# Reordering group 0 by hand and pairing the tiles of the two-chunk groups in a fused retention and snake-MLP kernel

## The chip, the cores and the metric

The kernel runs on one core of one Trainium2 chip. The metric is the device time in microseconds of one execution; ten runs of the kernel before are given by their median. Beside it stands one execution taken by the hardware profiler.

## The reference, cut to what matters

```python
# q, k, v: 4 batches, 8 heads, 768 steps, 64 wide
for t in range(S):
    state = gamma * state + k[:, :, t] (outer) v[:, :, t]
    y[:, :, t] = scale * q[:, :, t] @ state
x = y.transpose(0, 2, 1, 3).reshape(B * S, H * D)      # 3072 x 512
h = x @ w_in                                           # 512 x 2048
s = np.sin(alpha * h)
g = h + s * s / (alpha + 1e-09)
out = g @ w_out                                        # 2048 x 512
```

`gamma` is one decay factor per head, so that the recurrence can be worked in chunks of 128 steps: a masked product inside each chunk and a running state between chunks.

## The kernel before

**Tiles.** The 3072 rows are 24 chunks of 128 (four batches of six). `order` (L47) puts the first chunk of each batch in front, then the other chunks batch by batch; `P` is the same list, `e0` to `e3` are its first four. `sizes` (L49) cuts it into seven groups of 4, 2, 4, 4, 4, 4 and 2 chunks.

**Retention stages of a chunk j.** `stage_T` (L190) transposes q and k on TensorE and copies the result from PSUM to SBUF on DVE; for later chunks `turn` (L199) does this by a DMA transpose from SyncE's queue instead. `stage_A` (L204) makes the scores and DVE multiplies them by the mask (L214). `stage_M` (L233) makes the chunk's x from state and scores, adds to the state (`stage_S`, L217), and `keep_S` (L228) copies the state to SBUF with two ACT instructions. `scale_v` (L111) multiplies v by its decay, on DVE for a few chunks and on POOL for the others.

**MLP stages of a group g.** For each of 16 tiles f of the hidden width, `ff_in` (L262) runs four matmuls into a PSUM bank `ph`, then ACT's sine (L272) and a square (L274 on ACT, or L276 on DVE) and, when the returned function is called, DVE's add (L277), which makes `gT`. `ff_out` (L284) runs one matmul of 512 columns for one chunk ts and one f; after f = 15 it copies the 128x512 result with ACT and sends it out from SyncE's queue (L298).

**What sets the order.** The schedule is written out by hand (L60): each engine runs its instructions in the order in which the program emits them. `phase` (L357) emits for each f an `ff_in`, the retention stages attached to that f in `att`, the add, and a share of the output matmuls of the group before. Group 0 is written out (L391 to L454): its first six tiles f run for three chunks alone while the fourth chunk is still arriving, with the matmuls of `idle_work` (L307, on data that nobody reads) between; then the fourth chunk's 128 columns follow tile by tile; then ten tiles of all four chunks, with squares in turn on ACT and DVE. Output tile 0 trails them; the other three follow between the stages of chunks P[4] and P[5] (`fill`, L427). Then comes group 1's phase (L455), and the loop over groups 2 to 6 (L458).

**Banks and buffers.** PSUM is shared by tags: `mm` has four banks, for `ph`, `po` and early transposes; `ty`, `ps` and `pa` serve the retention stages. A new tile of a tag waits until the oldest one's readers are done. `s` has four buffers in SBUF.

**Loads.** Everything that needs a cast comes through POOL's DMA queue, in program order: first chunks, w_in and w_out in four pieces each (L117 to L125), chunks P[4] to P[6], then (L432) the other chunks, with the scaling of v between the loads. SyncE's queue holds the DMA transposes and the outputs.

```python
    for n in range(7, NJ + 3):
        if n > 8:
            scale_v(order[n - 3], nc.gpsimd)
        if n < NJ:
            load_chunk(order[n])
        if n in (13, 15, 17):
            scale_v(order[(n - 11) // 2], nc.gpsimd)
```

Of the kernel before, what the change touches and what calls it, by code (L numbers as in the profile page):

```python
# [15 lines left out]
def kernel(  # L16
# [15 lines left out]
    nc = tc.nc  # L32
# [40 lines left out]
    def load_chunk(j, names="qkv"):  # L73
        for name, src in (("q", q), ("k", k), ("v", v)):
            if name not in names:
                continue
            if name == "v":
                t = big.tile([128, H, D], BF16, name="vr", tag="vr", bufs=NJ)
            else:
                if ("qk", j) not in raw:  # L80
                    raw["qk", j] = big.tile([128, 2, H, D], BF16, name="qkr", tag="qkr", bufs=NJ)
                t = raw["qk", j][:, "qk".index(name)]
            nc.gpsimd.dma_start(out=t, in_=chunk_of(src, j))  # L83
            raw[name, j] = t
# [26 lines left out]
    def scale_v(j, eng):  # L111
        eng.tensor_mul(raw["v", j], raw["v", j], kg[:, j % NCH, :, None].to_broadcast([128, H, D]))  # L112
# [51 lines left out]
    def decay_table(c):  # L164
        nc.vector.tensor_mul(qg[:, c], qg[:, 0], step[:, c, :, None].to_broadcast([128, NP, C]))
# [21 lines left out]
        else:  # L187
            nc.vector.tensor_copy(o, pt)

    def stage_T(j):  # L190
        pt = psum.tile([128, 2 * NP, 128], BF16, name="pt", tag="ty")
        st["qkT", j] = work.tile([128, 2 * NP, 128], BF16, name="qkT", tag="qkT", bufs=6)
        for i in range(2):
            for p in range(NP):
                nc.tensor.transpose(pt[:, i * NP + p, :],
                                    raw["qk"[i], j][:, 2 * p:2 * p + 2, :].rearrange("p h d -> p (h d)"), ident)
        nc.vector.tensor_copy(st["qkT", j], pt)

    def turn(j):  # L199

# [3 lines left out]
    def stage_A(j):  # L204
        qkT = st["qkT", j]
        pa = psum.tile([128, 2, NP, 128], F32, name="pa", tag="pa")
        for p in range(NP):
            for e in range(2):
                r = slice(64 * e, 64 * e + 64)
                nc.tensor.matmul(pa[:, e, p, :], qkT[r, NP + p, :], qkT[r, p, :],  # L210
                                 start=(p == 0), stop=True, skip_group_check=True)
        aT = work.tile([128, 2, NP, 128], BF16, name="aT", tag="aT", bufs=2)
        m = dec.rearrange("p e n t -> p (e n) t") if j % NCH == 0 else mask_bc
        nc.vector.tensor_mul(aT.rearrange("p e n t -> p (e n) t"), pa.rearrange("p e n t -> p (e n) t"), m)  # L214
        st["aT", j] = aT
# [43 lines left out]

    gT = {}  # L260

    def ff_in(g, f, square, cols=None):  # L262
        n = sizes[g] * C
        lo, hi = cols or (0, n)
        if g not in gT:
            gT[g] = work.tile([128, FF, n], BF16, name="gT", tag="gT", bufs=2)
        ph = psum.tile([128, hi - lo], F32, name="ph", tag="mm", bufs=4)
        s = work.tile([128, hi - lo], F32, name="s", tag="s", bufs=4)
        for i in range(KS):
            nc.tensor.matmul(ph, w_in[:, i, f * 128:(f + 1) * 128], xT[g][:, i, lo:hi],  # L270
                             start=(i == 0), stop=(i == KS - 1))
        nc.scalar.activation(out=s, in_=ph, func=ACTF.Sin, scale=alpha_sb[:, f:f + 1])  # L272
        if square == "A":
            nc.scalar.activation(out=s, in_=s, func=ACTF.Square)  # L274
        else:
            nc.vector.tensor_mul(s, s, s)  # L276
        return lambda: nc.vector.scalar_tensor_tensor(  # L277
            gT[g][:, f, lo:hi], s, rec_alpha[:, f:f + 1], ph, op0=ALU.mult, op1=ALU.add)

    out_view = out.rearrange("(t p) n -> p t n", p=128)  # L280
    po = {}
    end = (NG - 1, sizes[-1] - 1)

    def ff_out(g, ts, f):  # L284
        if f == 0:
            po[g, ts] = psum.tile([128, d_model], F32, name="po", tag="mm", bufs=4)
        nc.tensor.matmul(po[g, ts], gT[g][:, f, ts * C:(ts + 1) * C], w_out[:, f, :],  # L287
                         start=(f == 0), stop=(f == FF - 1))
        if f == FF - 1:
            o_sb = work.tile([128, d_model], F32, name="o_sb", tag="o_sb", bufs=3)  # L290
            o_dram = out_view[:, groups[g][ts], :]
            if (g, ts) == end:
                h = d_model // 2
                nc.vector.tensor_copy(o_sb[:, :h], po[g, ts][:, :h])
                nc.scalar.copy(o_sb[:, h:], po[g, ts][:, h:])
            else:
                nc.scalar.copy(o_sb, po[g, ts])  # L297
            nc.sync.dma_start(out=o_dram, in_=o_sb)  # L298

    def out_pieces(g, tss):  # L300
        return [lambda ts=ts, f=f: ff_out(g, ts, f) for ts in tss for f in range(FF)]
# [5 lines left out]
    def idle_work(n):  # L307
        for _ in range(n):
            nc.tensor.matmul(spare["ps"], warm[:, :128], warm, start=True, stop=True)  # L309
# [41 lines left out]
    stage_M(e2)  # L351
    decay_table(2)
    idle_work(3)
    spare["ps"] = psum.tile([128, 512], F32, name="spare", tag="ps")


    def phase(g, outs, att, squares, slots=range(FF)):  # L357

        no, n0, done = len(outs), len(slots), 0
        for n, f in enumerate(slots):  # L360
            add = ff_in(g, f, squares[f % len(squares)])
            for fn in att.get(f, ()):
                fn()
            add()
            while done < no * (n + 1) // n0:
                outs[done]()
                done += 1

    def T(j):
        return lambda: stage_T(j)  # L370
# [7 lines left out]
    def M(j):  # L378
        return lambda: stage_M(j)

    def V(j):
        return lambda: scale_v(j, nc.vector)

    def G(c):
        return lambda: decay_table(c)

    def SK(j):
        return lambda: keep_S(j, stage_S(j))


    n3, early = 3 * C, 6  # L391
    adds = []
    for f in range(early):
        adds.append(ff_in(0, f, "AADAAA"[f], (0, n3)))
        if f == 0:
            decay_table(3)
        if f in (1, 2):
            adds.pop(0)()
        if f == 3:
            idle_work(2)  # L400
            stage_T(e3)
            idle_work(1)
            adds.pop(0)()
        if f == 4:
            stage_A(e3)
            adds.pop(0)()
    idle_work(2)
    adds.pop(0)()
    stage_M(e3)
    adds.pop(0)()  # L410
    idle_work(3)
    for f in range(early):
        add = ff_in(0, f, "AD"[f % 2], (n3, 4 * C))
        if f > 1:
            ff_out(0, 0, f - 2)
        add()
    decay_table(4)
    scale_v(e0, nc.vector)
    for t in s_bd:
        nc.vector.memset(t, 0.0)  # L420
    decay_table(5)
    P = order
    phase(0, [lambda f=f: ff_out(0, 0, f) for f in range(4, FF - 2)], {}, "AD", range(early, FF))
    outs = out_pieces(0, (1, 2, 3))
    outs[9:9] = [lambda f=f: ff_out(0, 0, f) for f in range(FF - 2, FF)]

    def fill(n):  # L427
        for _ in range(n):
            outs.pop(0)()


    for n in range(7, NJ + 3):  # L432
        if n > 8:
            scale_v(order[n - 3], nc.gpsimd)
        if n < NJ:
            load_chunk(order[n])
        if n in (13, 15, 17):
            scale_v(order[(n - 11) // 2], nc.gpsimd)

    fill(7)  # L440
    stage_T(P[4])
    scale_v(P[4], nc.vector)
    fill(5)
    stage_A(P[4])
    keep_S(P[0], stage_S(P[0]))
    fill(5)
    stage_T(P[5])
    scale_v(P[5], nc.vector)
    fill(5)
    stage_A(P[5])  # L450
    stage_M(P[4])
    fill(6)
    stage_M(P[5])
    fill(3)  # L454
    phase(1, outs,  # L455
          {0: [T(P[6]), X(P[8])], 2: [A(P[6])], 3: [T(P[7])], 4: [X(P[9])], 6: [A(P[7]), M(P[6])], 8: [X(P[10])],
           10: [A(P[8]), M(P[7])], 12: [X(P[11])], 13: [A(P[9]), M(P[8]), SK(P[9] - 1)], 15: [M(P[9])]}, "A")
    for g in range(2, NG):  # L458
        att = {}
        if g + 1 < NG:  # L460
            js = groups[g + 1]
            for i, j in enumerate(js):
                a = i * FF // len(js)
                n = P.index(j) + 2
                if n < NJ:
                    att.setdefault(a + 2, []).append(X(P[n]))
                att.setdefault(a + 1, []).append(A(j))
                if i > 0:
                    att[a + 1].append(M(js[i - 1]))
                if j % NCH == 1:  # L470
                    att[a + 1].append(SK(j - 1))
            att.setdefault(FF - 2, []).append(M(js[-1]))
        phase(g, out_pieces(g - 1, range(sizes[g - 1])), att, "A")
    for fn in out_pieces(NG - 1, range(sizes[-1])):
        fn()


# [1 line left out]
_INS = ['q', 'k', 'v', 'moe_w_in', 'moe_w_out', 'moe_alpha']  # L479
_OUTS = [((3072, 512), 'float32')]  # L480
# [25 lines left out]
```

## Time and profile before

| what | value |
|---|---|
| median of 10 runs | 222.1 us (221.55 to 222.6) |
| profiled execution | 222.06 us |
| its span, first to last instruction | 220.3 us, mean granted TensorE clock 0.998 |
| busy PE, weight load, DVE, ACT, POOL | 94, 48, 60, 75, 41% |
| output matmuls L287 | 96.3 us in 358 seen |
| input matmuls L270 | 101.5 us in 471 seen |
| add L277 | 75.7 us in 118 |
| sine L272, square L274 | 71.3 us in 118, 60.3 us in 109 |

A row of the profile's table of groups names line, engine, operation, output and inputs, count, busy time and mean of one. Matmuls are pipelined, so that the busy time of one (0.38 us for 512 columns) is longer than the distance between two; distances come from the chain of work that ended last, or from two starts. "Wait" is idle time of an engine, put down to what ended it.

### The profile page before, as it was taken

The page shows a single profiled execution, that of the slowest core. Times are in us where ns is not written, and L with a number is a line of the kernel's source. Part 1 is how long each engine was busy: PE and PEld are TensorE (multiplying, and loading weights), DVE is VectorE, ACT ScalarE, POOL GpSimd, SP SyncE. Part 2 cuts the span into 40 slices and gives each one's busy share as a digit, 9 for nine tenths or more (in the row PEclk, how much of TensorE's full clock was granted, in tenths as well). Part 3 has the DMA queues.
Part 4 walks back from the last instruction along what each step waited for, and adds up shares of the span by engine and source line. Part 5 has one row for each costly group of instructions (what it writes and reads, how often), then busy time and mean ns, then how long its engine had stood idle before and what let it go on. Part 6 is the DMA issues. An engine that isn't in the chain of part 4 may idle for free.

```text
span 220.3 us, 4253 instructions
## 1 busy us (share of the span) xinstructions
PE 206.1 (94%) x1632; PEld 106.7 (48%) x1661; DVE 132.8 (60%) x218; ACT 164.9 (75%) x322; POOL 90.1 (41%) x105
## 2 busy tenths in 40 slices
PE   7788889999999999999999999999999999999992
PEld 2444433457664545544455445455444444656540
DVE  5676798876896768854565555556554455333300
ACT  7778877538999999798778778778768877777720
POOL 8965335899999989799410000000000000000000
PEclk9999999999999999999999999999999999999999
DMA  8999999999999999999994247146111101111121
GB/s 124 153 189 190 206 207 162 155 197 150 202 135 158 147 148 182 156 173 137 147 139 70 28 95 72 28 97 72 26 49 51 48 0 51 48 48 48 52 87 56
DMA packets 99509, 24.67 MB, mean 112 GB/s; under 512 B 92304, under 2 KB 96416, under 8 KB 99488
## 3 DMA queue, kind: packets, MB, share of 16 engines
q0 software_dynamic: 77024, 13.37, 87.7%
q1 hardware_dynamic: 22464, 11.02, 27.3%
q8 instruction: 13, 0.21, 0.4%
q14 instruction: 8, 0.07, 0.1%
HBM read 27.27 MB, written 6.29 MB: 152 GB/s over the span
## 4 chain that ended last, share of the span: by engine, by line
PE 76%; DVE 8%; ACT 5%; DMA 4%; POOL 3%; issue 3%; POOLq 0%; ACTq 0%
PE po L287 35%; PE ph L270 32%; DMA w_in<-in_moe_w_in_dram 4%; DVE gT L277 3%; PE pa L210 3%; PE py L244 3%; ACT s L272 3%; PE py L248 2%; ACT s L274 2%; DVE aT L214 2%; POOL qkr L83 2%; POOL vr L83 1%; PE ps L224 1%; DVE s L276 1%; DVE xT L255 1%
## 5 line engine op out<-in xcount | busy, mean ns | idle before, releaser
L277 DVE SCALAR_TENSOR_TENSOR gT<-s,rec_alpha,ph 128x512 bf16<-128x512 f32 (+3 forms) x118 | 75.7, 645 | 67.3 <-ACT s L274 66.4
L270 PE MATMUL ph<-xT,w_in 128*128 128x512 bf16 (+3 forms) x471 | 101.5, 339 | 2.9 <-DVE gT L277 1.3
L287 PE MATMUL po<-w_out,gT 128*128 128x512 bf16 x358 | 96.3, 379 | 3.4 <-issue 2.1
L272 ACT ACTIVATE s<-ph,alpha_sb 128x512 f32<-128x512 f32 (+3 forms) x118 | 71.3, 606 | 32.5 <-PE ph L270 32.4
L270 PEld LDWEIGHTS <-w_in 128*128 128x128 bf16 x472 | 45.3, 98 | 47.4 <-issue 4.8
L274 ACT ACTIVATE s<-s 128x512 f32<-128x512 f32 (+3 forms) x109 | 60.3, 553 | 3.5
L287 PEld LDWEIGHTS <-gT 128*128 128x128 bf16 x384 | 35.5, 98 | 37.8 <-DVE gT L277 3.6
L112 POOL TENSOR_TENSOR vr<-vr,kg 128x512 bf16<-128x512 bf16 x21 | 22.3, 1071 | 9.0 <-DMA vr<-in_v_dram 9.0
L214 DVE TENSOR_TENSOR aT<-pa,mask 128x1024 bf16<-128x1024 f32 x20 | 24.4, 1221 | 0.1
L83 POOL DMA_DIRECT2D vr<-in_v_dram x24 | 21.8, 908 | 3.2 <-DMA w_in<-in_moe_w_in_dram 1.7
L83 POOL DMA_DIRECT2D qkr<-in_q_dram x23 | 21.3, 924 | 3.8 <-DMA w_in<-in_moe_w_in_dram 1.7
L83 POOL DMA_DIRECT2D qkr<-in_k_dram x23 | 20.5, 891 | 3.9 <-DMA w_out<-in_moe_w_out_dram 3.4
L297 ACT COPY o_sb<-po 128x512 f32<-128x512 f32 x23 | 13.2, 574 | 6.2 <-PE po L287 6.1
L231 ACT CAST s_bd<-ps 64x256 bf16<-64x256 f32 x40 | 14.4, 361 | 3.5 <-PE ps L224 2.9
L255 DVE TENSOR_TENSOR xT<-py,qg 128x512 bf16<-128x512 f32 x20 | 13.7, 683 | 2.3 <-PE py L248 2.2
L309 PE MATMUL spare<-warm 128*128 128x512 bf16 x34 | 11.1, 435 | 1.4 <-DVE warm L131 1.2
L248 PE MATMUL py<-aT,vr 128*64 128x128 bf16 x192 | 9.5, 219 | 0.5 <-DVE aT L214 0.4
L210 PE MATMUL pa<-qkT 64*128 64x128 bf16 x192 | 9.5, 219 | 0.4 <-ACT qkT L186 0.2
L210 PEld LDWEIGHTS <-qkT 64*128 64x128 bf16 x192 | 5.4, 94 | 9.2 <-issue 6.8
L244 PE MATMUL py<-qkT,s_bd 128*64 128x128 bf16 x160 | 8.3, 225 | 0.2 <-DVE xT L255 0.2
L248 PEld LDWEIGHTS <-vr 128*64 128x64 bf16 x192 | 6.9, 110 | 1.5 <-issue 1.1
L244 PEld LDWEIGHTS <-s_bd 128*64 128x64 bf16 x160 | 5.2, 109 | 4.0 <-issue 1.9
(58 smaller groups left out, 70.2 us busy)
## 6 DMA issues: line engine op xcount, KB each, us to landing
out_dram<-o_sb SPq DMA_DIRECT2D x24, 256.0 KB, 2.7
vr<-in_v_dram POOLq DMA_DIRECT2D x24, 128.0 KB, 7.2
qkr<-in_q_dram POOLq DMA_DIRECT2D x23, 128.0 KB, 7.8
qkr<-in_k_dram POOLq DMA_DIRECT2D x23, 128.0 KB, 7.4
w_in<-in_moe_w_in_dram POOLq DMA_DIRECT2D x4, 512.0 KB, 11.3
w_out<-in_moe_w_out_dram POOLq DMA_DIRECT2D x4, 512.0 KB, 14.9
q<-in_q_dram SPq DMA_DIRECT2D x1, 256.0 KB, 3.5
k<-in_k_dram SPq DMA_DIRECT2D x1, 256.0 KB, 4.2
```

The source lines that it names most:

```text
L83: nc.gpsimd.dma_start(out=t, in_=chunk_of(src, j))
L112: eng.tensor_mul(raw["v", j], raw["v", j], kg[:, j % NCH, :, None].to_broadcast([128, H, D]))
L210: nc.tensor.matmul(pa[:, e, p, :], qkT[r, NP + p, :], qkT[r, p, :], start=(p == 0), stop=True, skip_group_check=True)
L214: nc.vector.tensor_mul(aT.rearrange("p e n t -> p (e n) t"), pa.rearrange("p e n t -> p (e n) t"), m)
L244: nc.tensor.matmul(py[r, p, :], s_bd[c % 2][:, p, r], qkT[:, p, :], start=(p == 0), stop=True, skip_group_check=True)
L248: nc.tensor.matmul(py[64 * e:64 * e + 64, p, :], vs[:, 2 * p + e, :], aT[:, e, p, :], start=(c == 0 and p == 0), stop=True, skip_group_che ...
L255: nc.vector.tensor_mul(x, py, qg[:, c])
L270: nc.tensor.matmul(ph, w_in[:, i, f * 128:(f + 1) * 128], xT[g][:, i, lo:hi], start=(i == 0), stop=(i == KS - 1))
L272: nc.scalar.activation(out=s, in_=ph, func=ACTF.Sin, scale=alpha_sb[:, f:f + 1])
L274: nc.scalar.activation(out=s, in_=s, func=ACTF.Square)
L277: return lambda: nc.vector.scalar_tensor_tensor(gT[g][:, f, lo:hi], s, rec_alpha[:, f:f + 1], ph, op0=ALU.mult, op1=ALU.add)
L287: nc.tensor.matmul(po[g, ts], gT[g][:, f, ts * C:(ts + 1) * C], w_out[:, f, :], start=(f == 0), stop=(f == FF - 1))
```

## The change

- `ff_in` becomes a class `Slot`: building it emits the matmuls and sines of `nf` tiles f in one PSUM bank; `sq` emits one square over all of them, on ACT or DVE; `add` emits one add for each. `s` has five buffers.
- Group 0 is written out anew. All fillers in it go. Eight tiles f run for three chunks; each ACT square is emitted behind the next slot's sines. The fourth chunk's stages come after slots 3, 5 and 7 (stages T, A and M); its 128 columns follow as two slots of four tiles each. Output tiles 0 and 1 both trail the slots, in the banks of tags `ps` and `ty`. The tables and the scaling of e0 and the memsets move. P[4] and P[5] are transposed inside group 0, in `mm` banks, and copied by ACT instead of DVE.
- Of output tiles 2 and 3, 16 matmuls stand between groups 0 and 1 and 16 in group 1; before it were 31 and 19, of tiles 1 to 3 and the end of tile 0.
- On POOL, each scaling from chunk P[6] on comes one load earlier, and those of e1 to e3 move.
- `phase` squares on ACT alone. Groups 1 and 6, of two chunks, run in eight slots of two tiles f; `att` of group 1 is renumbered. Groups 2 to 5 keep their order.

```diff
+        def __init__(self, g, f, cols=None, nf=1, tag="mm"):
...
+            self.ph = psum.tile([128, nf, w], F32, name="ph", tag=tag, bufs=4 if tag == "mm" else 1)
+            self.s = work.tile([128, nf, w], F32, name="s", tag="s", bufs=5)
...
+            for m, f in enumerate(self.fs):
+                nc.scalar.activation(out=self.s[:, m, :], in_=self.ph[:, m, :], func=ACTF.Sin,
+                                     scale=alpha_sb[:, f:f + 1])
...
+        def sq(self, eng):
+            if eng == "A":
+                nc.scalar.activation(out=self.s, in_=self.s, func=ACTF.Square)
...
+        for n in range(FF // nf):
+            now = Slot(g, n * nf, nf=nf).sq("A")
+            for fn in att.get(n, ()):
                 fn()
-            add()
-            while done < no * (n + 1) // n0:
+            now.add()
+            while done < no * (n + 1) * nf // FF:
...
+    a = early(0)
+    decay_table(3)
     scale_v(e0, nc.vector)
     for t in s_bd:
         nc.vector.memset(t, 0.0)
+    b = early(1)
+    a.sq("A").add()
+    a = early(2)
+    b.sq("A")
+    c = early(3)
+    a.sq("A")
+    stage_T(e3)
+    b.add()
+    b = early(4, "ps")
+    c.sq("A")
+    a.add()
+    a = early(5)
+    b.sq("A")
+    stage_A(e3)
+    c.add()
+    c = early(6)
+    a.sq("A")
+    b.add()
+    b = early(7)
+    c.sq("A")
+    stage_M(e3)
+    b.sq("A")
+    a.add()
+    c.add()
+    po[0, 0] = psum.tile([128, d_model], F32, name="po", tag="ps")
+    po[0, 1] = psum.tile([128, d_model], F32, name="po", tag="ty")
+    F((0,), range(4))
+    F((1,), range(3))
+    b.add()
+    a = Slot(0, 0, (n3, n4), 4)
+    F((1,), (3,))
+    a.sq("A").add()
+    a = Slot(0, 8)
+    b = Slot(0, 4, (n3, n4), 4)
+    a.sq("A").add()
+    a = Slot(0, 9)
+    b.sq("D").add()
+    F((0, 1), (4,))
+    b = Slot(0, 10)
+    a.sq("A").add()
+    F((0, 1), (5,))
+    a = Slot(0, 11)
+    b.sq("D").add()
+    decay_table(4)
+    F((0, 1), (6, 7))
+    b = Slot(0, 12)
+    a.sq("A").add()
     decay_table(5)
...
+    b = Slot(0, 14)
+    a.sq("A").add()
+    F((0, 1), (10,))
+    stage_T(P[4], nc.scalar, "mm")
+    a = Slot(0, 15)
+    b.sq("D").add()
+    a.sq("A").add()
+    F((0, 1), (11, 12))
+    stage_A(P[4])
+    scale_v(P[4], nc.vector)
+    F((0, 1), (13, 14))
+    stage_T(P[5], nc.scalar, "mm")
+    F((0, 1), (15,))
...
+    load_chunk(P[7])
+    load_chunk(P[8])
+    scale_v(P[6], nc.gpsimd)
+    load_chunk(P[9])
+    scale_v(P[7], nc.gpsimd)
+    load_chunk(P[10])
+    scale_v(P[8], nc.gpsimd)
+    scale_v(e1, nc.gpsimd)
+    for n in range(11, NJ + 2):
+        scale_v(P[n - 2], nc.gpsimd)
+        if n < NJ:
+            load_chunk(P[n])
...
+    outs = out_pieces(0, (2, 3))
...
+    fill(3)
+    stage_A(P[5])
+    SK(e0)()
     scale_v(P[5], nc.vector)
     fill(5)
-    stage_A(P[5])
     stage_M(P[4])
-    fill(6)
+    fill(4)
     stage_M(P[5])
-    fill(3)
+    fill(4)
     phase(1, outs,
...
+          {0: [T(P[6]), X(P[8])], 1: [A(P[6])], 2: [T(P[7]), X(P[9])], 3: [A(P[7]), M(P[6])], 4: [X(P[10])],
+           5: [A(P[8]), M(P[7])], 6: [X(P[11]), A(P[9]), M(P[8]), SK(e1)], 7: [M(P[9])]}, 2)
```

More of the change, by code (lines that the diff above doesn't have):

```diff
@@ L188, in half_T, with stage_T @@
             nc.vector.tensor_copy(o, pt)
-    def stage_T(j):
-        pt = psum.tile([128, 2 * NP, 128], BF16, name="pt", tag="ty")
+    def stage_T(j, eng=None, tag="ty"):
+        pt = psum.tile([128, 2 * NP, 128], BF16, name="pt", tag=tag, bufs=4 if tag == "mm" else 1)
         st["qkT", j] = work.tile([128, 2 * NP, 128], BF16, name="qkT", tag="qkT", bufs=6)
@@ L196, in stage_T @@
                                     raw["qk"[i], j][:, 2 * p:2 * p + 2, :].rearrange("p h d -> p (h d)"), ident)
-        nc.vector.tensor_copy(st["qkT", j], pt)
+        if eng is nc.scalar:
+            nc.scalar.copy(st["qkT", j], pt)
+        else:
+            nc.vector.tensor_copy(st["qkT", j], pt)
     def turn(j):
@@ L260, with add @@
     gT = {}
[L262 to L278, printed above, removed]
+    class Slot:
+        def __init__(self, g, f, cols=None, nf=1, tag="mm"):
+            n = sizes[g] * C
+            self.lo, self.hi = cols or (0, n)
+            self.g, self.fs = g, range(f, f + nf)
+            if g not in gT:
+                gT[g] = work.tile([128, FF, n], BF16, name="gT", tag="gT", bufs=2)
+            w = self.hi - self.lo
+            self.ph = psum.tile([128, nf, w], F32, name="ph", tag=tag, bufs=4 if tag == "mm" else 1)
+            self.s = work.tile([128, nf, w], F32, name="s", tag="s", bufs=5)
+            for m, f in enumerate(self.fs):
+                for i in range(KS):
+                    nc.tensor.matmul(self.ph[:, m, :], w_in[:, i, f * 128:(f + 1) * 128], xT[g][:, i, self.lo:self.hi],
+                                     start=(m == 0 and i == 0), stop=(i == KS - 1), skip_group_check=True)
+            for m, f in enumerate(self.fs):
+                nc.scalar.activation(out=self.s[:, m, :], in_=self.ph[:, m, :], func=ACTF.Sin,
[3 more added lines that the diff above has]
+                nc.scalar.activation(out=self.s, in_=self.s, func=ACTF.Square)
+            else:
+                nc.vector.tensor_mul(self.s, self.s, self.s)
+            return self
+        def add(self):
+            for m, f in enumerate(self.fs):
+                nc.vector.scalar_tensor_tensor(gT[self.g][:, f, self.lo:self.hi], self.s[:, m, :], rec_alpha[:, f:f + 1],
+                                               self.ph[:, m, :], op0=ALU.mult, op1=ALU.add)
@@ L284, in ff_out @@
     def ff_out(g, ts, f):
-        if f == 0:
+        if (g, ts) not in po:
             po[g, ts] = psum.tile([128, d_model], F32, name="po", tag="mm", bufs=4)
@@ L289, in ff_out, with take @@
         if f == FF - 1:
[L290 to L298, printed above, removed]
+            take(g, ts)
+    def take(g, ts):
+        o_sb = work.tile([128, d_model], F32, name="o_sb", tag="o_sb", bufs=3)
+        if (g, ts) == end:
+            h = d_model // 2
+            nc.vector.tensor_copy(o_sb[:, :h], po[g, ts][:, :h])
+            nc.scalar.copy(o_sb[:, h:], po[g, ts][:, h:])
+        else:
+            nc.scalar.copy(o_sb, po[g, ts])
+        nc.sync.dma_start(out=out_view[:, groups[g][ts], :], in_=o_sb)
     def out_pieces(g, tss):
@@ L353, with phase @@
     idle_work(3)
[L354 to L362, printed above, removed]
-                fn()
-            add()
-            while done < no * (n + 1) // n0:
+    def phase(g, outs, att, nf=1):
+        no, done = len(outs), 0
+        for n in range(FF // nf):
+            now = Slot(g, n * nf, nf=nf).sq("A")
+            for fn in att.get(n, ()):
+                fn()
+            now.add()
+            while done < no * (n + 1) * nf // FF:
                 outs[done]()
@@ L379, in M, with F, early @@
         return lambda: stage_M(j)
[L381 to L385, printed above, removed]
     def SK(j):
         return lambda: keep_S(j, stage_S(j))
[L391 to L417, printed above, removed]
+    P = order
+    n3, n4 = 3 * C, 4 * C
+    def F(ts, fs):
+        for f in fs:
+            for t in ts:
+                ff_out(0, t, f)
+    def early(f, tag="mm"):
+        return Slot(0, f, (0, n3), tag=tag)
+    a = early(0)
+    decay_table(3)
     scale_v(e0, nc.vector)
@@ L420 @@
         nc.vector.memset(t, 0.0)
-    decay_table(5)
[L422 to L425, printed above, removed]
+    b = early(1)
[45 more added lines that the diff above has]
+    a.sq("A").add()
+    decay_table(5)
+    F((0, 1), (8,))
+    a = Slot(0, 13)
+    b.sq("D").add()
+    F((0, 1), (9,))
+    b = Slot(0, 14)
[3 more added lines that the diff above has]
+    a = Slot(0, 15)
+    b.sq("D").add()
+    a.sq("A").add()
[17 more added lines that the diff above has]
+            load_chunk(P[n])
+        if n in (13, 15):
+            scale_v(P[(n - 9) // 2], nc.gpsimd)
+    outs = out_pieces(0, (2, 3))
     def fill(n):
@@ L429, in fill @@
             outs.pop(0)()
[L432 to L447, printed above, removed]
+    fill(3)
+    stage_A(P[5])
+    SK(e0)()
     scale_v(P[5], nc.vector)
     fill(5)
-    stage_A(P[5])
     stage_M(P[4])
-    fill(6)
+    fill(4)
     stage_M(P[5])
-    fill(3)
+    fill(4)
     phase(1, outs,
-          {0: [T(P[6]), X(P[8])], 2: [A(P[6])], 3: [T(P[7])], 4: [X(P[9])], 6: [A(P[7]), M(P[6])], 8: [X(P[10])],
-           10: [A(P[8]), M(P[7])], 12: [X(P[11])], 13: [A(P[9]), M(P[8]), SK(P[9] - 1)], 15: [M(P[9])]}, "A")
+          {0: [T(P[6]), X(P[8])], 1: [A(P[6])], 2: [T(P[7]), X(P[9])], 3: [A(P[7]), M(P[6])], 4: [X(P[10])],
+           5: [A(P[8]), M(P[7])], 6: [X(P[11]), A(P[9]), M(P[8]), SK(e1)], 7: [M(P[9])]}, 2)
     for g in range(2, NG):
@@ L462 @@
             for i, j in enumerate(js):
-                a = i * FF // len(js)
+                a = i * FF // len(js) + 1
                 n = P.index(j) + 2
                 if n < NJ:
-                    att.setdefault(a + 2, []).append(X(P[n]))
-                att.setdefault(a + 1, []).append(A(j))
+                    att.setdefault(a + 1, []).append(X(P[n]))
+                att.setdefault(a, []).append(A(j))
                 if i > 0:
-                    att[a + 1].append(M(js[i - 1]))
+                    att[a].append(M(js[i - 1]))
                 if j % NCH == 1:
-                    att[a + 1].append(SK(j - 1))
+                    att[a].append(SK(j - 1))
             att.setdefault(FF - 2, []).append(M(js[-1]))
-        phase(g, out_pieces(g - 1, range(sizes[g - 1])), att, "A")
+        phase(g, out_pieces(g - 1, range(sizes[g - 1])), att, 1 if sizes[g] > 2 else 2)
     for fn in out_pieces(NG - 1, range(sizes[-1])):
```

## The prediction

> **What bounds the kernel now.** I read the page first (busy shares and slices), then a table of busy time by stretch, then the chain that ended last in order of time, then single engines in order of time. The stretches are cut where the work changes: first product with w_in (15.49), first full slots (27.0), stage A of the fifth chunk (42.77), group 1's first slot (49.9), group 2's first slot (67.85), last matmul (216.2).
>
> ```profile
> 15.49:27.00 11.51, 9.98 (x83) 5.75 (x86) 8.13 (x17) 8.70 (x21) 5.74 (x7) 1.00 1.51 195
> 27.00:42.77 15.77, 14.42 (x69) 5.81 (x68) 14.29 (x25) 10.17 (x18) 8.70 (x10) 1.00 1.91 177
> 42.77:49.90 7.13, 7.03 (x98) 4.11 (x100) 5.47 (x7) 3.07 (x8) 6.66 (x9) 1.00 2.06 188
> 49.90:67.85 17.95, 16.85 (x225) 12.09 (x227) 14.82 (x26) 16.31 (x42) 17.95 (x20) 1.00 1.94 163
> 67.85:216.20 148.35, 145.63 (x1061) 73.30 (x1079) 79.23 (x109) 114.57 (x207) 37.76 (x41) 1.00 0.90 86
> ```
>
> Columns after the length: busy us (and instructions) of PE, PE weight load, DVE, ACT, POOL, then granted clock, DMA share, GB/s. From 67.85 on PE is busy 145.63 of 148.35 us at clock 1.00; the chain there is 0.86 us pieces of four 512-column matmuls, 0.2155 each, end to end. That stretch cannot shorten unless matmuls go, and none go. So the change can only win or lose before 67.85, and what it wins reaches the end 1:1. Before that point the chain leaves PE:
>
> ```profile
> 28.00 0.60 DVE qg L165
> 28.61 0.60 DVE vr L112
> 29.21 0.27 DVE s_bd L420
> 29.48 0.27 DVE s_bd L420
> 29.76 0.54 DVE qg L165
> 30.30 0.65 DVE gT L277
> 30.95 0.61 DVE s L276
> ...
> 59.40 0.02 ACT s L274
> 59.42 0.30 issue
> 59.72 0.47 ACT s L272
> 60.21 0.43 ACT s L274
> ```
>
> In group 0 it sits on DVE: tables, a scaling and two memsets lie in front of the adds that free PE's banks. In group 1 it sits on ACT, sine after square.
>
> **What the reordered squares cost and save.** ACT, in order of time:
>
> ```profile
> 17.03 0.52 ACT L274 ACTIVATE s<-s 128x384 f32<-128x384 f32 x1
> 17.46 0.56 ACT L272 ACTIVATE s<-ph,alpha_sb 128x384 f32<-128x384 f32 x1
> 18.05 0.52 ACT L274 ACTIVATE s<-s 128x384 f32<-128x384 f32 x1
> ```
>
> An instruction that needs nothing from its neighbour starts 0.43 after it (17.03 to 17.46); a square of the sine just ahead starts 0.59 after it. A 384-column pair costs 1.02 now, and 0.88 with another sine between. For 256 columns the same reading (51.64, 52.14, 52.47) gives 0.50 + 0.33 = 0.83 a tile; a slot of two tiles is sine 0.33, sine 0.50, one 512-column square 0.55: 1.38 instead of 1.66.
>
> **15.49 to 24.25.** Slots 0 to 3 run as before, to 18.26. The fourth chunk's transposes then wait for its k, as now (done 19.95): the eight fillers that go lay in such waits, so they save nothing but the 0.2 before slot 4. Then PE has slots 4 to 7 (0.65 each) and stage A (0.33): 22.9. DVE is later than that: copy of the transposes from 20.15, 0.69; two adds of 0.53; mask product 1.22: 23.1. Stage M follows; ACT's copy of its result comes behind square 6: about 24.95. The first output tile's bank is slot 4's, free after two more adds, 24.2, so its first product runs at 24.25 (now 24.43), but with eight slots done for three chunks, not six.
>
> **24.25 to 42.2.** PE: 32 output products up to f=15 for two tiles, two quads (16 matmuls of 128 columns, 0.055 each), eight full slots 0.86, transposes 2 x 0.45, A 0.33. Products trail the adds, so weights decide little: by their issue times and times to landing, w_in pieces 2 and 3 land at 25.6 and 30.7, w_out 1 to 3 at 28.2, 33.3, 35.8; I reach slot 8 at 26.9, slot 12 at 33.1, f=12 at 39.7. PE would reach slot 15 at 37.3, but its bank is slot 12's. DVE from the first quad's square (28.6): four 128-column adds 1.1; wait for square 8 until 30.75; then adds 8 to 12 at 0.66, two squares of full tiles and one of a quad at 0.63, a quad's adds 1.1, two tables at 0.63: 7.5, so 38.3. Slot 15 waits 1.1. Then 0.86 + four products 0.86 + A 0.33 = 40.45 (now 42.77, with the same 26 output products behind it); four products, transposes, two products: 42.2. The scaling and memsets moved to the front run in 16.1 to 17.3, where DVE now waits 1.45 for the first square.
>
> **42.2 to group 1.** Here ACT gets work DVE had: two copies of 128x1024 transposes. No row has one; 128x512 takes 0.586, so between 0.59 and 1.17; I take 1.1, as cost per column dominates in the ACT rows. Behind the second copy (to 43.05) queue both output copies (0.55 each, 44.15), and behind those the state copies: 0.75, M 0.82, 0.75, M 0.82: 47.3 (at 0.59 the start would be 0.5 earlier). Four trailing products and the last x: group 1 starts at 48.25, not 49.9, and with 48 output products behind it, not 45.
>
> **Group 1.** PE: 64 products 6.9, 16 outputs 3.45, transposes 0.9, four A 1.3, four M with state 3.3, one more state 0.15, issue gaps 0.6: 16.6. ACT: 8 x 1.38 + five state copies 0.74 + up to two output copies 0.57 = 15.9. DVE: adds 16 x 0.44, four mask products 1.13, four x and two transposes at 0.6: 15.1. Now ACT's sum is 16 x 0.83 + 3.7 + 1.1 = 18.1, which is the 17.95 seen. Three engines near 16 will not mesh perfectly: I take 17.1, between the floor 16.6 and today's 17.95. Group 2 then starts at 65.35, 2.5 earlier.
>
> **Queues.** SP: the turns of chunks 8 and 9 move from slots 0 and 4 of 16 to 0 and 2 of 8, and the third tile's output stands ahead of the first turn, so chunk 8 turns at about 49.4 (now 48.22). Chunk 9's k lands at 46.08 + 5.65 = 51.7 and it turns then, as it no longer stands behind the output at 53.87. The turns took 5.7, 6.9, 8.6 and 9.3 to land: 55.1 to 58.7 for chunk 8, whose A is due near 57.3, 58.7 to 61 for chunk 9, due near 60.5. No wait is likely, a short one possible. POOL: each scaling comes one load earlier and waits for it, so two chunks are in flight, not three: load 11 goes out 2 us later (54.6), then about one load in 5 us instead of 3.7. PE takes a chunk in 8 us after 67.85, so that costs nothing; without that reserve it would cost all of 1.3 us a chunk.
>
> **Nothing elsewhere.** In groups 2 to 5 instructions stay in order. In group 6 ACT saves 8 x 0.28, but PE is dense (0.43 + 0.86 a tile), and ACT has slack. A fifth s buffer frees nothing PE waits for.
>
> **Clock.** The fillers kept PE busy. The row that prices losing it: the first nine fillers took 3.68 us, 0.41 each, against 0.217 later (five in 1.25). The Trainium skill, "TensorE: Matmul & The Clock Gate", section "Part 1: The HAM clock gate", has the array fall to half rate after an idle window of about 3.4 us. By that rule the change costs 0, as my longest gap is 1.7 us with transposes inside it; if sparse work counted as idle, the first row's price is half of 3.7 us, 1.8, for each such window. I take 0 and keep 0 to 3.6.
>
> **Sum.** Profiled execution: 222.06 us, span 220.3, 1.76 around it. 222.06 - 2.5 = 219.6; I round for a short turn wait to 219.7. The median before is 222.1, practically the same.
>
> **Rivals.**
> - Better (0.10): group 1 at 16.6, the copy at its low end and slot 15 unheld (1.1): up to 2.5 + 0.5 + 0.5 + 1.1 = 4.6, less overlap: 217.5 to 218.5.
> - Group 1 does not shorten (0.22): DVE's adds in pairs behind one square replace ACT as its bound, 17.95 again: start 66.2, 220.4. For: DVE there is busy 14.82. Against: its sum is 3 us under ACT's now.
> - Turns late (0.12): landing in 10.9 us, the slowest in this trace, puts chunk 9's A at 62.6, and from A to group 2 is about 4.2 (now 3.94): 66.8 to 67.5, so 221.0 to 221.8.
> - Slower (0.11): the clock. In 18.3 to 24.3 the slots wait for chunk, adds and banks; if PE falls to half for two windows, 3.6 is lost against 2.5 won: 223.2. It decides once more than 2.5 us go, that is 5 us of matmuls at half clock. Against it: the gaps are short.
> - That squares behind sines bring nothing in group 0 is partly in the forecast: there PE, chunk and DVE set the time, not ACT.
>
> The likeliest case has 0.45 and 218.6 to 220.4. The range 218.0 to 222.3 takes in late turns and leaves out most of the clock case and the lower half of the better one. A measurement can tell about 0.2% (0.44 us) from no change: faster 0.81, same 0.08, slower 0.11.
>
> **What would show it.** Right: group 2's first product at 65 to 66 with granted clock 1.00 throughout; from there to the last matmul 148.3 again; A of the fifth chunk near 40.5; slot 15 waiting on a DVE add; ACT near 15.5 busy in group 1. Wrong: transposes or A waiting for the turn's DMA; clock under 1.00 or 0.41 us matmuls in 18 to 28; group 1 still 18 long; a wait on POOL's scalings after group 2 starts.

## The result and the profile after

The changed kernel takes 219.49 us (median), the kernel before 222.12 us beside it: a ratio of 0.9881 with a 95% interval of 0.9864 to 0.9899, so 2.6 us or 1.2% less. The forecast was 219.7. The profiled execution took 219.49 us with a span of 217.7.

The busy time by stretch, cut at first product with w_in, first output product, stage A of the fifth chunk, first product of group 1, of group 2, last matmul. The second cut differs from that of the table of before, which has the first full slot there; the others are the same events. Columns: length, then busy us of PE, weight load, DVE, ACT, POOL, then granted clock, DMA share, GB/s.

```profile
15.40:24.03 8.63, 6.94 (x56) 3.90 (x57) 6.40 (x13) 6.66 (x15) 4.08 (x6) 1.00 1.60 191
24.03:40.27 16.24, 15.31 (x96) 7.74 (x99) 12.26 (x24) 12.33 (x26) 7.88 (x10) 1.00 1.69 188
40.27:48.41 8.14, 7.70 (x101) 4.51 (x103) 6.50 (x8) 4.65 (x10) 7.20 (x9) 1.00 2.26 186
48.41:65.28 16.87, 15.62 (x221) 12.01 (x224) 14.04 (x25) 14.37 (x33) 15.26 (x17) 1.00 2.04 158
65.28:213.60 148.32, 145.68 (x1062) 73.25 (x1079) 78.93 (x110) 112.79 (x200) 42.38 (x46) 1.00 0.79 89
```

Read it against the lines of before, the last two above all. Group 1 starts at 48.41 instead of 49.90 (1.49 won), and lasts 16.87 instead of 17.95 (1.08 won). That is 2.57 of the 2.6. From group 2's first product to the last matmul it is 148.32 against 148.35: nothing won, nothing lost. ACT's busy time in group 1 fell from 16.31 to 14.37 while PE's share of the stretch stayed nearly the same (94%, now 93%). ACT has 9% of the chain in group 1 instead of 20%. The end of that chain, from 58.70 on, is DVE's work but for short issue times:

```profile
62.08 1.13 DVE aT L217
63.22 0.60 DVE xT L258
63.81 0.78 DVE gT L294 x2
64.59 0.65 DVE xT L258
65.24 0.04 issue
65.28 0.81 PE ph L279 x3
```

The chain that ended last, around the end of group 0 (start, length, what):

```profile
21.09 16.88 DMA qkr<-in_k_dram
37.97 0.05 issue
38.01 0.40 PE pt L195 x4
38.41 0.04 issue
38.45 1.02 PE ph L279 x4
39.47 0.86 PE po L304 x4
40.34 0.33 PE pa L213 x8
```

This is the one piece that I did not have. In this chain no DVE piece is left ahead of slot 15 (38.45); what stands there is a load: the fifth chunk's k, issued at 21.09 and landed at 37.97. Its transposes stand in front of slot 15 on PE. DVE in the same place (start, length, operation):

```profile
36.93 0.68 DVE L289 TENSOR_TENSOR s<-s 128x512 f32<-128x512 f32 x1
37.65 1.41 DVE L294 SCALAR_TENSOR_TENSOR gT<-s,rec_alpha,ph 128x512 bf16<-128x512 f32 x2
```

The first of the two adds is slot 12's, which frees slot 15's bank. One such add takes 0.75 us here, so it ends at about 38.4, where the forecast had 38.3. The transposes behind the load end at 38.4 too. So slot 15 waits for two things that end within 0.1 us of each other, and a chain can name only one.

### The profile page after: what moved, and what is told of

Read it like the earlier page. It is cut to its first block, busy times and chain, and to the rows that moved or that the text cites. A ratio compares the mean times of both kernels' runs of the same rounds, so it can differ in the third digit from the quotient of the medians.

```text
span 217.7 us, 4218 instructions
## 1 busy us (share of the span) xinstructions
PE 204.4 (94%) x1634; PEld 107.9 (50%) x1661; DVE 128.6 (59%) x213; ACT 162.8 (75%) x311; POOL 90.0 (41%) x105
## 4 chain that ended last, share of the span: by engine, by line
PE 73%; DMA 12%; POOL 4%; DVE 4%; issue 3%; ACT 2%; POOLq 0%
PE po L304 34%; PE ph L279 30%; DMA qkr<-in_k_dram 8%; DMA w_in<-in_moe_w_in_dram 4%; PE py L247 3%; PE pa L213 2%; POOL qkr L83 2%; PE py L251 2%; DVE aT L217 1%; POOL vr L83 1%; DVE xT L258 1%; PE ps L227 1%; DVE gT L294 1%; PE pt L195 1%; ACT s L282 1%
## 5 line engine op out<-in xcount | busy, mean ns | idle before, releaser
L294 DVE SCALAR_TENSOR_TENSOR gT<-s,rec_alpha,ph 128x512 bf16<-128x512 f32 (+3 forms) x120 | 74.1, 637 | 68.2 <-ACT s L287 67.6
L279 PE MATMUL ph<-xT,w_in 128*128 128x512 bf16 (+3 forms) x478 | 97.9, 336 | 0.8 <-DVE gT L294 0.2
L304 PE MATMUL po<-w_out,gT 128*128 128x512 bf16 x360 | 94.1, 379 | 3.8 <-issue 2.8
L282 ACT ACTIVATE s<-ph,alpha_sb 128x512 f32<-128x512 f32 (+3 forms) x120 | 69.6, 602 | 34.0 <-PE ph L279 33.8
L287 ACT ACTIVATE s<-s 128x512 f32<-128x512 f32 (+1 forms) x94 | 58.4, 621 | 2.6
L328 PE MATMUL spare<-warm 128*128 128x512 bf16 x27 | 9.7, 483 | 1.4 <-DVE warm L131 1.2
```

Source lines behind the costliest of these rows:

```text
L279: nc.tensor.matmul(self.ph[:, m, :], w_in[:, i, f * 128:(f + 1) * 128], xT[g][:, i, self.lo:self.hi], start=(m == 0 and i == 0), stop=(i = ...
L282: nc.scalar.activation(out=self.s[:, m, :], in_=self.ph[:, m, :], func=ACTF.Sin, scale=alpha_sb[:, f:f + 1])
L287: nc.scalar.activation(out=self.s, in_=self.s, func=ACTF.Square)
L294: nc.vector.scalar_tensor_tensor(gT[self.g][:, f, self.lo:self.hi], self.s[:, m, :], rec_alpha[:, f:f + 1], self.ph[:, m, :], op0=ALU.mult ...
```

## The experiments

My theory after the result: about 1.5 us come from group 0 (eight slots instead of six before the fourth chunk, two tiles trailing, DVE's long queue broken up; these were not tested apart) and about 1.1 from pairing in group 1, where ACT was the bound. The rivals: one of the two parts is the whole gain; the order of the squares makes it; the fillers held the clock; POOL's reorder counts. A second question was what holds slot 15. Medians of before beside the runs were 222.06 (first set), 222.05 (second) and 222.32 (third); each ratio is to the one of its own set.

One thing moves the profiled executions whatever the edit. The fourth chunk's k, issued at 9.97 to 10.02 us, landed between 18.54 and 20.53 in the six executions of the changed kernel and its edits whose chain shows it, and the first output product follows it by 4.45 or 4.46 us in all six of them. So profiled executions are compared here by lengths, or from the first output product on (24.43 in the kernel before, 24.03 in the changed one), and not by their times on the clock.

**Pairing alone**, in the kernel before:

```diff
-    phase(1, outs, {0: [T(P[6]), X(P[8])], 2: [A(P[6])], ...}, "A")
+    phase2(1, outs, {0: [T(P[6]), X(P[8])], 1: [A(P[6])], ...})   # two tiles f a slot; group 6 too
```

> The kernel before, with only the pairing: groups 1 and 6 in eight slots of two tiles f. My theory: group 1 has 19 output products here, so PE's own work in it is 16.6 + 3 x 0.2155 = 17.25 us against 17.95 now; group 1 shortens by 0.3 to 0.7 us and group 6 by nothing: 221.4 to 221.8 us. Rival (the pairing is the gain, as ACT was the bound of group 1): ACT's sum falls from 18.1 to 15.9, so 1.5 us or more: 220.6 or less.

Measured: 221.56 us, ratio 0.9971 (0.9955 to 0.9987), 0.5 less. Group 1 ran from 50.29 to 67.42, 17.13 instead of 17.95 (it started late because the first output product came at 24.82):

```profile
50.29:67.42 17.13, 16.94 (x228) 12.27 (x227) 14.04 (x25) 14.14 (x33) 17.13 (x19) 1.00 1.93 157
```

The pairing does take ACT's bound away, but with 19 output products left PE's own work (my 17.25, slightly too much) becomes the next one at once: it is busy 16.94 of the 17.13 us.

**The changed kernel without pairing:**

```diff
-        phase(g, out_pieces(g - 1, range(sizes[g - 1])), att, 1 if sizes[g] > 2 else 2)
+        phase(g, out_pieces(g - 1, range(sizes[g - 1])), att)          # and sixteen slots in group 1
```

> The changed kernel, with groups 1 and 6 back in sixteen slots of one tile. My theory: group 1 goes back from 16.87 to about 17.8 us (ACT's sum 18.1, part of it running over into group 2): 220.2 to 220.6 us, that is 0.7 to 1.1 more than the changed kernel. Rival (group 0 is the whole gain): within 0.3 of the changed kernel's 219.5. Rival (pairing is the whole gain): back at 222.

Measured: 220.56 us, ratio 0.9927 (0.9899 to 0.9954). Group 1 lasted 17.94 us (49.28 to 67.22), though it had three output products fewer than the kernel before in its 17.95. With one tile a slot, ACT is as busy as before (16.43 us, then 16.31), the chain runs through its sines and squares and the DVE work behind them, and PE's smaller load is lost. The row of group 1, and PE's waits near its end and at the start of group 2:

```profile
49.28:67.22 17.94, 16.77 (x225) 11.77 (x224) 14.77 (x26) 16.43 (x42) 16.21 (x19) 1.00 1.87 163
```

```profile
62.69 0.60 PE L279 MATMUL ph<-xT,w_in 128*128 128x256 bf16 x4 [0.50 <-DVE gT L294]
...
67.22 1.02 PE L279 MATMUL ph<-xT,w_in 128*128 128x512 bf16 x4 [0.49 <-DVE xT L258]
```

So neither part is the whole: 0.5 for pairing alone, 1.5 for group 0 alone, 2.6 for both. The sum of the parts is 0.6 short of the whole by the medians and 0.4 by the ratios, which the intervals do not tell from chance. The lengths of group 1, in one execution each, show some of it: against 17.95 before, pairing alone wins 0.82, three output products fewer alone 0.01, and both together 1.08. So in these traces 0.25 us of PE's smaller load count only once ACT is out of the way.

**Squares straight behind their own sines in group 0**, as an example of the edit:

```diff
-    b = early(1)
-    a.sq("A").add()
+    b = early(1).sq("A")
+    a.add()
```

> The changed kernel, with each square of group 0 straight behind its own sine again. My theory: the x of the fourth chunk and the second tile's first products come 0.4 to 0.5 us later, but slot 15 and what follows wait for the transposes of the fifth chunk, whose k lands at 38.0 us whatever the order, so nearly all of it is swallowed: 219.4 to 219.9 us. Rival (the order of the squares is what group 0 gains by): 0.14 us for each of 16 slots and the quads, 1.1 to 2.2 us: 220.6 to 221.7.

Measured: 219.16 us, ratio 0.9872 (0.9842 to 0.9901): not slower than the changed kernel. In the profiled execution, 220.44 us, k landed at 39.2 and slot 15 started at 39.48, right behind its transposes. Slots 8 and 14 do start later there (27.21 and 37.02 instead of 26.65 and 35.75, with the first output product at 24.05), and the wait ahead of slot 15 takes that up. The order of the squares is worth nothing in the time that these runs can show; the interval leaves room for about 0.6 us.

**The kernel before without fillers** (the eight `idle_work` matmuls of group 0 deleted):

> The kernel before, without the eight fillers of group 0 (matmuls on data that nobody reads). My theory: they lay in waits for the fourth chunk, adds and w_out, and the clock stays at 1.00: 221.8 to 222.2 us, group 2's first product at 67.6 to 67.9. Rival (they hold the clock): part of the matmuls from 18 to 28 us at 0.41 us each, 1.8 us for each window: 223.5 or more.

Measured: 222.09 us, ratio 1.0 (0.9979 to 1.0021). In 18 to 24 us PE's busy time falls from 5.20 to 3.61. First the row of before, then that of this run:

```profile
18.00:24.00 6.00, 5.20 (x46) 2.63 (x46) 5.12 (x9) 4.64 (x10) 3.89 (x5) 1.00 1.38 201
```

```profile
18.00:24.00 6.00, 3.61 (x43) 2.27 (x43) 4.99 (x9) 4.63 (x10) 4.11 (x5) 1.00 1.31 206
```

The granted clock of 1.00 cannot settle the matter alone, as that column reads 1.00 in the first 4 us of the kernel before too, where nine fillers take 0.41 us each:

```profile
0.00:4.00 4.00, 2.81 (x7) 1.01 (x8) 2.16 (x24) 2.98 (x8) 3.17 (x9) 1.00 0.52 113
```

```profile
1.19 3.68 PE L309 MATMUL spare<-warm 128*128 128x512 bf16 x9 [1.19 <-DVE warm L131]
```

The lengths of the matmuls settle it. Four of 384 columns take 0.81 us with the fillers, and 0.81 without:

```profile
20.16 0.81 PE L270 MATMUL ph<-xT,w_in 128*128 128x384 bf16 x4
```

```profile
19.66 0.81 PE L270 MATMUL ph<-xT,w_in 128*128 128x384 bf16 x4
```

That ends the rival that was to make the kernel slower: in this run PE, 60% busy with gaps of up to 0.72 us, kept its rate, and the interval has no room for even one window's 1.8 us.

**The old order on POOL** in the changed kernel:

```diff
-    scale_v(P[8], nc.gpsimd)
-    scale_v(e1, nc.gpsimd)
-    for n in range(11, NJ + 2):
-        scale_v(P[n - 2], nc.gpsimd)
+    for n in range(7, NJ + 3):
+        if n > 8:
+            scale_v(order[n - 3], nc.gpsimd)     # e1 behind load 13 again
```

> The changed kernel, with the old order on POOL: each scaling one load later, that of e1 behind load 13 of the order. My theory: the scaling of e1 ends at about 63.6 us as in the kernel before, and the state step that needs it, now at 61.8, waits for it; the output products behind it on PE wait too: 1.5 to 1.9 us more, 221.0 to 221.4 us. Rival (POOL's order is free, or three chunks in flight even help): 219.2 to 219.6.

Measured: 221.31 us, ratio 0.9977 (0.996 to 0.9994): nearly the whole gain is gone. The profiled execution is one of the faster ones, 220.79 us. Its group 1 lasts 18.34 us (48.23 to 66.57), and PE shows why, in two lines of its order of time:

```profile
61.28 0.40 PE L213 MATMUL pa<-qkT 64*128 64x128 bf16 x8 [0.59 <-DMA qkT<-qkr]
...
63.49 0.32 PE L227 MATMUL ps<-vr,qkr 128*64 128x64 bf16 x8 [1.25 <-POOL vr L112]
```

The first wait is the turn of P[9] (the rival "turns late", in small): with the old order of loads the turns between 45 and 70 us took 7.8 to 10.3 us to land, in the changed kernel 5.5 to 8.0. The second is the state step that needs e1's scaled v, which POOL finishes at 63.4. That was early enough for the old group 1 and is too late for the new one.

**Slot 15's two bounds.** Five edits of the changed kernel: tables 4 and 5 moved on DVE behind the sixth chunk's stage M; the fifth chunk's transposes moved behind slot 15; both; and, once the first runs were read, the fifth chunk's loads moved ahead of the last piece of w_out, alone and with the late tables.

```diff
-    decay_table(4)          # among the adds of group 0; table 5 likewise
...
     stage_M(P[5])
+    decay_table(4)
+    decay_table(5)
```

> The changed kernel, with decay tables 4 and 5 moved on DVE from among the adds of group 0 to behind the sixth chunk's stage M, where DVE is idle for 1.7 us. It takes 1.3 us out of DVE's queue ahead of the add that frees slot 15's bank. Theory A (the fifth chunk's k, landing at 38.0, holds slot 15, which stands behind its transposes on PE): 219.3 to 219.6 us, no change. Theory B (as I forecast, DVE's add holds slot 15): up to 1.1 us less, 218.4 to 218.9.

Measured: 218.64 us, ratio 0.9855 (0.9831 to 0.988).

```diff
-    stage_T(P[4], nc.scalar, "mm")
     a = Slot(0, 15)
...
+    stage_T(P[4], nc.scalar, "mm")
     F((0, 1), (11, 12))
+    F((0, 1), (13,))
     stage_A(P[4])
```

> The changed kernel, with the transposes of the fifth chunk emitted behind slot 15 instead of ahead of it (its stage A two output products later). Theory A (k's landing holds slot 15): slot 15 starts about 1 us earlier, 218.5 to 219.0 us. Theory B (the add of slot 12, done at 38.3, holds it): slot 15 still starts at 38.4: 219.3 to 219.7. Both bounds lie 0.1 us apart, so I expect B's number here and A's in the run with late tables alone.

Measured: 219.39 us, ratio 0.988 (0.986 to 0.99). The time is what I expected, but slot 15 did not stay at 38.4:

```profile
37.23 1.03 PE L279 MATMUL ph<-xT,w_in 128*128 128x512 bf16 x4
38.64 0.38 PE L195 MATMUL pt<-ident,qkr 128*128 128x128 bf16 x4 [0.39 <-DVE gT L294]
39.25 0.40 PE L195 MATMUL pt<-ident,qkr 128*128 128x128 bf16 x4 [0.23 <-DMA qkr<-in_k_dram]
```

My expectation overlooked that the transposes take a bank of `mm` as well. Emitted behind slot 15, they leave it slot 11's bank and take slot 12's themselves. So this edit freed slot 15 of both bounds and put both on the transposes; it does not tell one from the other.

> The changed kernel with both edits: tables 4 and 5 late on DVE, transposes of the fifth chunk behind slot 15. If both bounds hold slot 15 at the same moment, only this run moves: slot 15 at 37.1 instead of 38.45, 0.5 to 1.0 us less at the end: 218.5 to 219.0 us. If a later wait (two ACT copies of the transposes, the output copies and the state copies behind them) takes their place: 219.3 to 219.6.

Measured: 219.46 us, ratio 0.9874 (0.985 to 0.9898). My expectation of a gain here failed. Slot 15 does start at 37.38, again in slot 11's bank, but the transposes then cost their 0.45 us in the open instead of in the wait, and stage A waits for ACT's copy of them, which now stands behind slot 15's sine and square:

```profile
37.38 1.03 PE L279 MATMUL ph<-xT,w_in 128*128 128x512 bf16 x4
38.24 0.61 PE L195 MATMUL pt<-ident,qkr 128*128 128x128 bf16 x8
38.69 1.46 PE L304 MATMUL po<-w_out,gT 128*128 128x512 bf16 x6
40.74 0.40 PE L213 MATMUL pa<-qkT 64*128 64x128 bf16 x8 [0.60 <-ACT qkT L198]
```

Nearly all of the 1.07 us by which slot 15 comes earlier than in the changed kernel's profile is given back as 0.45 + 0.60. And in the run with late tables alone, which I had expected to show no change, k landed early in the profiled execution (37.2), slot 15 followed it at once, and the first output product had come at 22.66, 1.4 us ahead of the changed kernel's; whether the add, that landing or the start made the gain, one run could not say. So the last set has a control on the same chip.

> The changed kernel once more, unaltered, as the control beside the next three: 219.2 to 219.8 us. The fifth chunk's k should land between 37 and 39.3 us, as in the runs so far, and slot 15 should follow the later of that landing's transposes and slot 12's add (38.3).

> Tables 4 and 5 late on DVE, as before, beside its control on one chip. Theory (slot 15 waits for two things that end within 0.2 us of each other, the fifth chunk's k and slot 12's add): taking away the add's part gains only in executions in which k lands ahead of 38 us, so 0 to 0.9 us less than the control, about 0.4. Theory B (the add alone holds it): 0.9 us less throughout.

> The changed kernel with the fifth chunk's three loads issued ahead of the last quarter of w_out instead of behind it, tables where they are. Its k should land 2 us or more earlier, the last w_out piece about 2 us later (38), just ahead of f=12. Theory of two bounds: slot 15 then waits for slot 12's add alone, 38.3: 0 to 0.3 us less than the control. If k alone holds slot 15: about 1 us less.

> Both: the fifth chunk loaded ahead of the last quarter of w_out, tables 4 and 5 late. Theory of two bounds: slot 15 starts at about 37.4 with no wait, 0.9 to 1.1 us less than the control in every execution: 218.3 to 218.7 us. If the last w_out piece becomes the wait (f=12 at 38.3 or later), half of it: 218.8 to 219.2.

```diff
-    load_w_out(3)
-    for j in order[4:7]:
+    load_chunk(order[4])
+    load_w_out(3)
+    for j in order[5:7]:
```

| kernel | median us | ratio (95%) | slot 15 starts at, in the profiled execution, and what held it |
|---|---|---|---|
| control | 219.11 | 0.9862 (0.9838 to 0.9887) | 38.43, add of slot 12 |
| tables late | 218.85 | 0.9845 (0.9824 to 0.9866) | 37.89, no wait of its own left; k's landing (37.61) is ahead of its transposes |
| fifth chunk early | 219.16 | 0.9853 (0.983 to 0.9877) | 38.91, add of slot 12 |
| both | 218.12 | 0.983 (0.9806 to 0.9854) | 36.59, no wait of its own left |

The same executions, counted from the first output product:

| kernel | first output product | from it to slot 15 | to group 1 | length of group 1 |
|---|---|---|---|---|
| control | 24.01 | 14.42 | 24.30 | 16.88 |
| tables late | 24.17 | 13.72 | 23.77 | 16.87 |
| fifth chunk early | 24.50 | 14.41 | 24.29 | 16.87 |
| both | 22.99 | 13.60 | 23.50 | 17.29 |

The chain of the control ahead of slot 15, where the two tables (L165) are still on it:

```profile
35.13 0.60 DVE qg L165
35.73 0.66 DVE gT L294
36.39 0.60 DVE qg L165
36.99 0.61 DVE s L289
37.60 0.03 issue
37.63 0.76 DVE gT L294
38.39 0.04 issue
38.43 1.02 PE ph L279 x4
```

PE in the kernel with early loads alone and in the one with both, one fence each:

```profile
37.50 0.61 PE L196 MATMUL pt<-ident,qkr 128*128 128x128 bf16 x8
38.91 1.02 PE L280 MATMUL ph<-xT,w_in 128*128 128x512 bf16 x4 [0.80 <-DVE gT L295]
```

```profile
35.99 0.61 PE L196 MATMUL pt<-ident,qkr 128*128 128x128 bf16 x8
36.59 1.02 PE L280 MATMUL ph<-xT,w_in 128*128 128x512 bf16 x4
```

With the load out of the way alone, the add still holds slot 15 for 0.80 us, and the distance is the control's. It is 14.42 in the changed kernel's first profile too, where the chain named the load, and 14.42 and 14.41 in those with POOL's old order and without pairing. So in these five executions the add that the forecast named sets slot 15. The load is a second bound close to it: it decides where it lands later, as in the run with the other order of squares (39.2).

Late tables alone shorten the way to slot 15 by 0.70, both edits by 0.82. At group 2's first product, 0.54 us is left of the first and 0.39 of the second: with both, the two tables behind stage M delay DVE's first work for group 1, which lasts 17.29 us instead of 16.88. These are single executions. The one with both was 1.43 us faster than the control's, but 1.02 of this is its start, as the fourth chunk's k landed at 18.54 instead of 19.56. No run shows that the edit causes this: with early loads alone it landed at 20.04. In the medians, tables late are 0.3 and both edits 1.0 under the control, with overlapping intervals. So the version with both beats the kernel before (1.7% less, 1.5 to 1.9); that it beats the changed kernel, and that it takes both edits, is not shown.

Keeping group 6 alone unpaired was not tried. But the kernel without pairing has it unpaired, and from group 2's first product to the end of the last matmul (67.22 to 215.54) it takes 148.32 us too, so the pairing of group 6 brings nothing that shows.

## Why the prediction was right

- **Where the gain can lie.** Before 67.85 only, and 1:1 from there: 2.57 won by then, 2.6 in all.
- **15.49 to 24.25.** First output product at 24.03, forecast 24.25, with eight slots done. The whole start was 0.09 earlier in this execution.
- **24.25 to 42.2.** Stage A of the fifth chunk at 40.27, forecast 40.45. The reason given, slot 12's add at 38.3, holds: that add ends at 38.4, and slot 15 keeps its distance from the first output product when the load is moved away. What the forecast left out is a second bound that nearly ties with it. I listed when the pieces of w_in and w_out land, and not the fifth chunk's k, which stands behind them in the same queue. The profile of before has it: issued at 21.22 and 16.6 to landing, 37.8, with its transposes not until 41.15, so 3.3 us of slack that the change uses up. That it did not land later, as in one run here, was luck.
- **ACT's copies.** 1.01 us for 128x1024, taken as 1.1; stage A of the sixth chunk at 43.19, forecast behind a copy that ends at 43.05; group 1 at 48.41, forecast 48.25.
- **Group 1.** 16.87, taken as 17.1 between 16.6 and 17.95. It is 16.87 or 16.88 in every kernel here that keeps the change's pairing and POOL order, but for the last one. ACT fell further than forecast (14.37 us busy, forecast near 15.5). PE is busy 93% of it, close to its own work, and DVE carries the end of the chain: the rival that put DVE in ACT's place as the bound came true in part, but it did not keep the group at 17.95.
- **Squares.** The distance of an ACT pair with another sine between fell as read off: 17.39, 17.80, 18.26 are 0.41 and 0.46, a pair of 0.87 (forecast 0.88). That it would bring little in group 0 was the last rival in the list, and the runs show no gain from it.
- **Queues.** The turns were in time, as said. POOL's new order I costed as a loss hidden by a reserve, and gave it no credit. It is a condition of the gain: left as before, it takes back 1.8 us of the median (1.3 in the profiled execution). The forecast came out right because the change contained it, not because I had priced it.
- **Clock.** Nothing was lost, as forecast: the kernel before kept its time and the lengths of its matmuls without fillers, and the changed kernel has none in group 0. The price of 1.8 us for each window was never paid. The sign that I named, a granted clock of 1.00, would not have shown a loss, as it reads 1.00 over the slow first fillers too; the other, matmuls of 0.41 us, would.

## What to carry to other kernels

When a stage is made faster, list every load and every helper queue whose result it consumes, with its landing time, and compare it with the new due time: slack that was 3 us wide can be the next bound. A wait may have two causes that end together; the chain names one. Measure the wait from an earlier event of the stage, take each cause away in turn, and see with which the distance changes. Count from such an event whenever two profiled executions are compared, as a load that lands 1 us earlier looks like a gain. And check which buffer an instruction gets after it is moved: the edit may take away more than it was meant to. Two changes on engines that bound the same stage in turn can be worth more together than the sum of each alone.

## What the runs showed of the hardware

The landing of one and the same load wanders. The fourth chunk's k landed anywhere from 18.54 to 20.53 us, as said above, and the time moves with it: in the kernel with early loads it came 0.48 us later than in the control, and the execution took 0.47 us longer. The fifth chunk's k, issued near 21 us behind the weights, landed at 37.2 to 39.2.

A DVE product of two SBUF operands takes 0.68 us, but took 1.43 in the changed kernel where POOL was scaling another chunk. Line 112 on both engines, in the changed kernel's order of time:

```profile
44.60 1.04 POOL L112 TENSOR_TENSOR vr<-vr,kg 128x512 bf16<-128x512 bf16 x1 [0.48 <-DMA vr<-in_v_dram]
```

```profile
44.77 1.43 DVE L112 TENSOR_TENSOR vr<-vr,kg 128x512 bf16<-128x512 bf16 x1
```

POOL's ends at 45.64; 0.56 us later, at 46.20, DVE's does, as if it had begun when POOL was done. The runs vary the overlap by chance. In eight of their traces DVE's product begins within POOL's, takes between 0.85 and 1.51 us, and ends 0.55 or 0.56 after POOL's in all of them. In the kernel with early loads alone DVE began first; its product took 0.68 and POOL's was the long one:

```profile
45.23 0.68 DVE L112 TENSOR_TENSOR vr<-vr,kg 128x512 bf16<-128x512 bf16 x1
```

```profile
45.35 1.45 POOL L112 TENSOR_TENSOR vr<-vr,kg 128x512 bf16<-128x512 bf16 x1 [0.39 <-ACT s_bd L235]
```

The Trainium skill, "SBUF — State Buffer", section "SBUF: two separate sides", tells of a port pair that the two engines lock for a whole instruction, whichever starts first; the nine traces agree. The late tables grew too in the kernel with both edits, to 1.31 and 1.52 us: the second ends 0.55 after a product on POOL, and what held the first is open.
